# One fused attention and ELU kernel: four PSUM tiles for the first layer of batch 0, full-width stationary blocks, and issues in other slots

## The chip, the cores and the metric

The kernel runs on one core of a Trainium2 chip. Its time is device microseconds of one execution: 360.8 us is the median of three runs (360.18 to 362.03). Lower is better. The engines are PE (TensorE matmuls; PEld are its weight loads), DVE (VectorE), ACT (ScalarE), POOL (GpSimd) and SP (which here only issues DMAs).

## The reference: what is computed

```python
B, H, S, D = 8, 8, 576, 64                 # q, k, v
scores = q @ k.T / sqrt(D) - slope[h] * |i - j|     # slope[h] = 2 ** -(h + 1)
scores = where((i - j >= 0) & (i - j < 128), scores, -1e9)
attn = softmax(scores)                     # exp / sum
x = (attn @ v) as [B*S = 4608, H*D = 512]  # tokens x model
h = x @ w_in                               # [4608, 2048]
g = where(h > 0, h, exp(min(h, 0)) - 1)    # ELU
out = g @ w_out                            # [4608, 512], float32
```

Each query sees itself and the 127 keys before it, so attention is a band: 128 keys meet at most 256 queries.

## The kernel before

Everything runs on PE in float16 with float32 sums. The program is one long list of instructions in an order written out by hand; each engine takes its own instructions in that order and waits on semaphores for the others. The order comes from a loop over **slots** (L430): in slot s stand first what `before(s, ...)` has put there (exponentials on ACT), then `hidden(s)`, then `elu(s-1)`, then what `at(s, ...)` has put there (attention steps, loads, transposes), then `output` if the slot has one.

Attention of batch b (576 positions, 8 heads) is cut into key blocks u = 0 to 3 of 128 keys, of which the last also takes the 64 keys of block 4:

- `load_qk`, `load_v`, `load_wi`, `load_wo` issue DMAs on POOL's queue (they cast to float16); the first two load a batch, the others the weights.
- `turn_qk` transposes q and k on DVE (`QT`, `KT`). Batch 0 is done by `turn_first` instead: PE transposes into PSUM, copied out by DVE (k) and ACT (q).
- `scores(b, u)` multiplies key block u (stationary) with its 256 queries into `sp`, one PSUM tile of four banks, two heads a bank. For u = 3 it takes 192 queries for block 3 and then 64 for block 4, whose stationary block is 64 wide. In batch 0 the ALiBi bias is added by further matmuls (`SI`, `RB`); in the others the exponentials are multiplied by a table.
- `expo` takes exp from `sp` to `EX` on ACT; `weigh` multiplies `EX` with `TAB` on DVE (not in batch 0).
- `values(b, i, gp)` multiplies the weights of query block i (stationary, from `EX`) with `VP`, four heads at a time, into `av`; a column of ones in `VP` gives the denominator. DVE takes its reciprocal (L197) and multiplies (L198) into `xn`. Query block 4 has 64 queries, so there the stationary block is 64 wide, and one of its two parts has 64 rows.
- `turn` transposes `xn` into `xT`, by PE and DVE (batches 0 and 1 for the most part) or by a DMA of SP's queue.

The two layers take 512 tokens t at a time. `hidden(t, c0, w, f0, nf)` fills one PSUM bank `hp` with 512 columns of the first layer (16 matmuls with 128 tokens, 8 with 256), ACT takes exp into `e` (L230), POOL clips it (L231), and `elu` on DVE makes `g` from `e` and `hp` (L238), after which the bank is free. `hp` has two buffers, taken in turn by all of `hidden`. `output(t, ts, f0)` adds four matmuls of the second layer (128 tokens x 512) to a bank `op`; after the fourth such step ACT copies it to `ob` (three buffers) and SP stores it.

Slots 0 to 15 are `hidden` of t = 0 together with batch 0's attention, slots 16 and 17 the first 64 tokens of t = 1, slots 18 to 33 `output` of t = 0 with no `hidden` at all, slots 34 to 47 the rest of t = 1 with batch 1's attention; from there on each slot has a `hidden` and an `output`. Batch b from 2 on starts at slot `START[b]` (41, 57, 75, 93, 111, 129); its `values(b, 4, 0)` and `values(b, 4, 1)` stand 17 and 18 slots later, its `turn_qk` in the 8 slots before it starts.

PSUM's eight banks: four for `sp`, two for `hp`, one for `av` (also used as `output`'s ts = 1 in t = 0), one for `op` (also `xps`).

## Time and profile before

| | |
|---|---|
| median of three runs | 360.8 us (360.18 to 362.03) |
| the profiled execution | 360.57 us, of which the span on the page is 358.8 |
| PE busy | 332.8 us (93%), 3706 matmuls |
| DVE, ACT, POOL busy | 223.3 (62%), 175.4 (49%), 172.8 us (48%) |
| `hidden` on PE (L225) | 1600 matmuls |
| `output` on PE (L247) | 576 matmuls |
| `values` on PE (L189) | 576 matmuls, 128 of them with a 64-wide stationary block |
| `scores` on PE (L167, batches 1 to 7) | 560 matmuls, 112 of them with a 64-wide one |

How the rows are read. A row of a timeline is: start in us, busy us, engine, line, operation, out<-in, the stationary block (rows*columns), the shape, a count of equal instructions merged, and in brackets how long the engine had been idle before and what ended that. Matmuls are pipelined and the ends are modelled: eight matmuls merged can show 1.04 us and the next row start 0.87 us after this one, so a cost on PE is the distance between starts. A row of stretches gives busy time with the number of instructions for PE, PEld, DVE, ACT and POOL, then the clock granted to TensorE, the mean busy share of the DMA engines, and GB/s.

### The profile page before, as it was taken

What the parts mean: (1) busy time and instruction counts of PE and PEld (TensorE: products, weight loads), DVE (VectorE), ACT (ScalarE), POOL (GpSimd) and SP (SyncE); (2) the same over time, 40 slices, a digit from 0 to 9 for tenths busy, and PEclk for the clock granted to TensorE, in tenths of its full rate; (3) what the DMA queues carried; (4) which work ended last, traced back from release to release, by engine and by line L of the source; (5) the groups of instructions that cost most, each with busy time, mean ns of one, the idle gap of its engine ahead of it and who ended that gap; (6) DMA issues with size and microseconds to landing.
All of it is one profiled execution on the core that took longest, in us unless ns stands there. A gap on an engine that the chain in (4) does not pass through costs nothing.

```text
span 358.8 us, 8891 instructions
## 1 busy us (share of the span) xinstructions
PE 332.8 (93%) x3706; PEld 230.7 (64%) x3706; DVE 223.3 (62%) x443; ACT 175.4 (49%) x313; POOL 172.8 (48%) x261
## 2 busy tenths in 40 slices
PE   8898879856999999999999999999999999999994
PEld 8687664445676666766667666666677666666641
DVE  5445536479668866786669756786679566654320
ACT  1645344554455545554666255555556365533421
POOL 9336459254466536562666456562656133332320
PEclk9879999999999999999999999999999999999999
DMA  9998349995577838994899649991999311111011
GB/s 111 195 188 110 36 41 134 190 151 38 65 107 94 91 64 104 107 97 69 93 112 94 78 67 123 100 98 39 136 115 102 61 45 46 46 45 38 29 60 58
DMA packets 97320, 32.10 MB, mean 89 GB/s; under 512 B 87040, under 2 KB 92672, under 8 KB 97280
## 3 DMA queue, kind: packets, MB, share of 16 engines
q0 software_dynamic: 76480, 18.36, 60.2%
q1 hardware_dynamic: 20800, 13.18, 13.1%
q8 instruction: 29, 0.48, 0.5%
q14 instruction: 11, 0.09, 0.1%
HBM read 36.70 MB, written 9.44 MB: 129 GB/s over the span
## 4 chain that ended last, share of the span: by engine, by line
PE 68%; DVE 10%; ACT 8%; DMA 4%; issue 4%; POOL 4%; ACTq 0%; DVEq 0%; POOLq 0%
PE hp L225 26%; PE op L247 25%; PE av L189 9%; DVE g L238 5%; ACT EX L173 5%; PE sp L167 4%; POOL e L231 3%; ACT e L230 3%; DMA wo<-in_moe_w_out_dram 2%; DMA out_dram<-ob 2%; PE spare L257 2%; DVE EX L179 2%; DVE KT L127 1%; PE sp L148 1%; DVE QT L127 1%
## 5 line engine op out<-in xcount | busy, mean ns | idle before, releaser
L231 POOL TENSOR_SCALAR e<-e 128x512 f32<-128x512 f32 x144 | 93.5, 650 | 167.1 <-ACT e L230 166.3
L225 PE MATMUL hp<-xT,wi 128*128 128x256 f16 (+3 forms) x1600 | 151.0, 243 | 12.8 <-DVE g L238 9.4
L225 PEld LDWEIGHTS <-wi 128*128 128x128 f16 x1600 | 122.3, 98 | 52.4 <-issue 17.3
L247 PE MATMUL op<-wo,g 128*128 128x512 f16 x576 | 145.3, 379 | 2.6 <-ACT ob L251 1.4
L230 ACT ACTIVATE e<-hp 128x512 f32<-128x512 f32 x144 | 87.2, 605 | 115.0 <-PE hp L225 112.6
L238 DVE SCALAR_TENSOR_TENSOR g<-e,hp 128x512 f16<-128x512 f32 x144 | 96.9, 673 | 55.9 <-POOL e L231 54.4
L247 PEld LDWEIGHTS <-g 128*128 128x128 f16 x576 | 50.7, 97 | 48.2 <-issue 7.8
L173 ACT ACTIVATE EX<-sp 128x512 f16<-128x512 f32 (+1 forms) x121 | 69.8, 634 | 15.9 <-PE sp L167 10.1
L179 DVE TENSOR_TENSOR EX<-EX,TAB 128x1024 f16<-128x1024 f16 x56 | 39.1, 699 | 29.5 <-ACT EX L173 29.5
L189 PE MATMUL av<-VP,EX 128*128 128x65 f16 (+1 forms) x576 | 44.4, 200 | 2.5 <-ACT EX L173 1.3
L189 PEld LDWEIGHTS <-EX 128*128 128x128 f16 (+1 forms) x576 | 34.7, 100 | 12.6 <-issue 3.1
L251 ACT COPY ob<-op 128x512 f32<-128x512 f32 x36 | 21.1, 586 | 40.6 <-PE op L247 38.4
L198 DVE TENSOR_TENSOR xn<-av,rden 128x256 f16<-128x256 f32 (+1 forms) x80 | 33.8, 423 | 2.7
L93 POOL DMA_DIRECT2D VP<-in_v_dram x40 | 35.0, 879 | 0.7 <-issue 0.6
L197 DVE RECIPROCAL rden<-av 128x4 f32<-128x4 f32 (+1 forms) x80 | 14.1, 176 | 24.1 <-PE av L189 23.9
L127 DVE STREAM_TRANSPOSE KT<-st 128x576 f16<-128x576 f16 x28 | 22.5, 814 | 0.0
L127 DVE STREAM_TRANSPOSE QT<-st 128x576 f16<-128x576 f16 x28 | 22.3, 807 | 0.0
L167 PE MATMUL sp<-QT,KT 32*128 32x256 f16 (+2 forms) x560 | 18.3, 250 | 2.7 <-ACT EX L173 2.7
L87 POOL DMA_DIRECT2D st<-in_q_dram x28 | 19.1, 681 | 2.7 <-DMA wo<-in_moe_w_out_dram 2.1
L87 POOL DMA_DIRECT2D st<-in_k_dram x28 | 19.2, 689 | 0.7 <-DMA VP<-in_v_dram 0.6
L167 PEld LDWEIGHTS <-KT 32*128 32x128 f16 (+1 forms) x560 | 10.5, 95 | 5.9 <-issue 4.2
L257 PE MATMUL spare<-ident 128*128 128x128 f16 x90 | 6.6, 249 | 1.6 <-DVE ident L282 1.6
(33 smaller groups left out, 60.8 us busy)
## 6 DMA issues: line engine op xcount, KB each, us to landing
out_dram<-ob SPq DMA_DIRECT2D x36, 256.0 KB, 2.4
VP<-in_v_dram POOLq DMA_DIRECT2D x32, 128.0 KB, 4.0
st<-in_k_dram POOLq DMA_DIRECT2D x28, 144.0 KB, 3.6
st<-in_q_dram POOLq DMA_DIRECT2D x28, 144.0 KB, 3.5
wi<-in_moe_w_in_dram POOLq DMA_DIRECT2D x4, 512.0 KB, 11.1
wo<-in_moe_w_out_dram POOLq DMA_DIRECT2D x4, 512.0 KB, 6.1
VP<-in_v_dram POOLq DMA_DIRECT2D x8, 64.0 KB, 3.2
xT<-xn SPq DMA_TRANSPOSE x32, 3.4
```

The source lines that it names most:

```text
L87: nc.gpsimd.dma_start(st[b][32 * g:32 * g + 32, w, :, :, :, :].rearrange("p h n j d -> p (h n) (j d)"), (q, k)[w][b, 2 * g:2 * g + 2, :, : ...
L93: nc.gpsimd.dma_start(VP[b % 2][0:p, n, :, 0:D], v[b, :, 128 * n:128 * n + p, :].rearrange("h p d -> p h d"))
L127: V.transpose(o, st[b][:, w, h2, :, :, 32 * dh:32 * dh + 32])
L167: nc.tensor.matmul(sp[0:m, g, 256 * h2 + o:256 * h2 + o + n], kt[r, h2, dh, 128 * kb:128 * kb + m], qt[r, h2, dh, q0:q0 + n], start=dh == ...
L173: nc.scalar.activation(unit(b, u)[:, g0:g1, :, c0:c1], sp[:, g0:g1, :].rearrange("p g (h c) -> p g h c", h=2)[:, :, :, c0:c1], AF.Exp, sca ...
L179: V.tensor_tensor(out=e, in0=e, in1=TAB[:, int(u == 3), 2 * gp:2 * gp + 2, :, :], op=ALU.mult)
L189: nc.tensor.matmul(a[0:m, g, h2, :], e[0:kk, 2 * gp + g, h2, c:c + m], VP[b % 2][0:kk, n, 4 * gp + 2 * g + h2, 0:D + 1], start=j == 0, sto ...
L225: nc.tensor.matmul(p[:, l * w + u0:l * w + u1], w_in_sb[:, c, fc * 128:(fc + 1) * 128], xT[:, c, x0:x0 + u1 - u0], start=(c == 0), stop=(c ...
L230: nc.scalar.activation(e[:, 0:n], p[:, 0:n], AF.Exp)
L231: nc.gpsimd.tensor_scalar(out=e[:, 0:n], in0=e[:, 0:n], scalar1=1.0, scalar2=0.0, op0=ALU.min, op1=ALU.max)
L238: V.scalar_tensor_tensor(out=gs[t][:, f0:f0 + nf, c0:c0 + w], in0=sh(es.pop((t, c0, f0))), scalar=1.0, in1=sh(hps.pop((t, c0, f0))), op0=A ...
L247: nc.tensor.matmul(o, gs[t][:, fc, ts * 128:(ts + 1) * 128], w_out_sb[:, fc, :], start=(fc == 0), stop=(fc == NFC - 1))
```

## The change

It has four parts, all in the program's text below.

1. **PSUM.** `sp` becomes a two-bank tile `spa` and two one-bank tiles; `hp` becomes two named tiles. `hidden` is told its tile: in slots 0 to 3 `hp[0]` and `hp[1]` in turn, in slots 4 to 15 those two and `sp[2]`, `sp[3]`, four in turn, in slots 16 and 17 `sp[2]` and `sp[3]`. In slots 34 to 39 three in turn (`hp[0]`, `hp[1]` and the one of `op`), after that two as before. `e` has six buffers instead of three. Batch 1's PE transposes of `turn` use the bank of `av` instead of that of `op`.
2. **Batch 0's scores by four heads.** `first_scores(u, half, d)` does four heads into two banks, and `first_expo` takes their exponentials in pieces, one of 512 elements or two of 256, instead of one of 1024.
3. **Stationary blocks all 128 wide.** `KT` and `EX` are 64 columns longer and zeroed there, `VP`'s rows 64 to 127 of block 4 are zeroed, and `scores` and `values` always take 128 rows or columns. The rows that are not wanted are not read.
4. **Other slots.** The second part of `turn_first` (96 transposes) goes from the prologue into slot 0; block 1's scores are in front of slot 0's `hidden`; `load_wo(0)` and `load_wo(1)` follow the last `load_wi` in the prologue, `load_wo(2)` and `load_wo(3)` stand in slots 15 and 16, batch 1's loads a little earlier.

```diff
-    ps_h = ctx.enter_context(tc.tile_pool(name="ps_h", bufs=2, space=PSUM))
+    ps_h = ctx.enter_context(tc.tile_pool(name="ps_h", bufs=1, space=PSUM))
...
-    KT = [one([128, 2, 2, S], F16, f"KT{i}") for i in range(2)]
+    kt_ = [one([128, 4 * S + 64], F16, f"KT{i}") for i in range(2)]
+    KT = [t[:, 0:4 * S].rearrange("p (a b s) -> p a b s", a=2, b=2) for t in kt_]
-    EX = [one([128, 4, 2, 256], F16, f"EX{i}") for i in range(4)]
+    ex_ = [one([128, 2048 + 64], F16, f"EX{i}") for i in range(4)]
+    EX = [t[:, 0:2048].rearrange("p (g h c) -> p g h c", g=4, h=2) for t in ex_]
-    sp = ps_s.tile([128, 4, 512], F32, name="sp", tag="sp")
+    spa = ps_s.tile([128, 2, 512], F32, name="spa", tag="spa")
+    sp = [spa[:, 0, :], spa[:, 1, :]] + [ps_s.tile([128, 512], F32, name=f"sp{i}", tag=f"sp{i}") for i in (2, 3)]
+    hp = [ps_h.tile([128, 512], F32, name=f"hp{i}", tag=f"hp{i}") for i in range(2)]
...
+        def blocks(u):
+            return [(0, u, 128 * u, 256)] if u < 3 else [(0, 3, 384, 192), (192, 4, 512, 64)]
+        def first_scores(u, half, d):
+            heads = [(x, hh) for x in (2 * half, 2 * half + 1) for hh in range(2)]
+            for part, (o, kb, q0, n) in enumerate(blocks(u)):
+                for x, hh in heads:
+                    c = 256 * (x % 2) + o
+                    nc.tensor.matmul(sp[2 * d + hh][:, c:c + n], SI[:, 4 * hh + x, :], RB[:, 0:n],
+                                     start=part == x % 2 == 0, stop=False, skip_group_check=True)
+            for o, kb, q0, n in blocks(u):
+                for x, hh in heads:
+                    r, c = slice(64 * hh, 64 * hh + 64), 256 * (x % 2) + o
+                    k0 = x * S + 128 * kb
+                    nc.tensor.matmul(sp[2 * d + hh][:, c:c + n], kt_[0][r, k0:k0 + 128], Q0[r, x, q0:q0 + n],
+                                     start=False, stop=True, skip_group_check=True)
+        def first_expo(u, half, d, c0, c1):
+            if d == 0:
+                nc.scalar.activation(
+                    unit(0, u)[:, half::2, :, c0:c1],
+                    spa.rearrange("p g (h c) -> p g h c", h=2)[:, :, :, c0:c1], AF.Exp, scale=0.125)
+                return
+            for hh in range(2):
+                nc.scalar.activation(
+                    unit(0, u)[:, half + 2 * hh, :, c0:c1],
+                    sp[2 + hh].rearrange("p (h c) -> p h c", h=2)[:, :, c0:c1], AF.Exp, scale=0.125)
...
         def scores(b, u):
+                            k0 = (2 * h2 + dh) * S + 128 * kb
-                                sp[0:m, g, 256 * h2 + o:256 * h2 + o + n], kt[r, h2, dh, 128 * kb:128 * kb + m],
+                                sp[g][:, 256 * h2 + o:256 * h2 + o + n], kt_[b % 2][r, k0:k0 + 128],
         def values(b, i, part):
-                        nc.tensor.matmul(
-                            a[0:m, g, h2, :], e[0:kk, 2 * gp + g, h2, c:c + m],
-                            VP[b % 2][0:kk, n, 4 * gp + 2 * g + h2, 0:D + 1],
+                    for j, (u, c, n) in enumerate(parts):
+                        c += 512 * g + 256 * h2
+                        nc.tensor.matmul(a[:, x, h2, :], ex_[u][:, c:c + 128], VP[b % 2][:, n, 2 * g + h2, 0:D + 1],
...
-            e = es[t, c0, f0] = work.tile([128, 512], F32, name="e", tag="e")
+            e = es[t, c0, f0] = work.tile([128, 512], F32, name="e", tag="e", bufs=6)
...
+            V.memset(VP[i][64:128, 4, :, 0:D], 0.0)
+            V.memset(kt_[i][:, 4 * S:4 * S + 64], 0.0)
+        for e in ex_:
+            V.memset(e[:, 2048:2112], 0.0)
...
+        load_wo(0)
+        load_wo(1)
...
+        BUF = [hp[0], hp[1], sp[2], sp[3]]
+            HID[s] = [(0, 128 * sub, 128, 4 * f, 4, BUF[s % 2 if s < 4 else s % 4])]
+            HID[16 + f] = [(1, 0, 64, 8 * f, 8, BUF[2 + f])]
+            HID[s] = [(1, *step, (hp[0], hp[1], None)[(s - 34) % 3] if s < 40 else BUF[s % 2])]
+                HID[16 * t + 16 + j] = [(t, 256 * (j // 8), 256, 2 * (j % 8), 2, BUF[j % 2])]
...
+        at(0, turn_first, 1, 1, 0, hp[1])
+        at(0, values, 0, 1, 0)
+        at(0, turn_first, 0, 1, 0, None)
...
-        at(0, load_wo, 0)
-        at(2, load_wo, 1)
-        at(17, load_wo, 2)
-        at(18, load_v, 1, 0)
-        at(19, load_v, 1, 1)
-        at(20, load_wo, 3)
-        for n in range(3):
-            at(21 + n, load_v, 1, 2 + n)
+        at(15, load_wo, 2)
+        at(16, load_wo, 3)
+        for n in range(5):
+            at(17 + n, load_v, 1, n)
```

Three places in the built order. First PE at the end of `values(2, 4, 0)` and the `output` behind it, as at every batch's query block 4 (`EX_92` is key block 3's weights, `VP_87` the even batches' values); of the eight pairs the last three stand here. Before:

```order
L189 LDWEIGHTS EX_92
L189 MATMUL av<-VP_87,EX_92 64x65
L189 LDWEIGHTS EX_92
L189 MATMUL av<-VP_87,EX_92 64x65
L247 LDWEIGHTS g
L247 MATMUL op<-wo,g 128x512
```

After:

```order
L206 LDWEIGHTS EX_92
L206 MATMUL av<-VP_87,EX_92 128x65
L206 LDWEIGHTS EX_92
L206 MATMUL av<-VP_87,EX_92 128x65
L267 LDWEIGHTS g
L267 MATMUL op<-wo,g 128x512
```

Nothing moved here; the outputs have 128 rows instead of 64, the same eight matmuls stand in the same place.

Second DVE from slot 9 to slot 18, where `elu` frees the tiles of `hidden` (`hp_99` and `hp_100` are the two of `hp`, `sp_97` and `sp_98` the two taken from the scores). Before:

```order
L238 SCALAR_TENSOR_TENSOR g<-e,hp 128x4x128
L197 RECIPROCAL rden<-av 64x4
L198 TENSOR_TENSOR xn<-av,rden 64x256
L238 SCALAR_TENSOR_TENSOR g<-e,hp 128x4x128
L211 COPY xT<-xps 128x4x64
L238 SCALAR_TENSOR_TENSOR g<-e,hp 128x4x128 x7
L238 SCALAR_TENSOR_TENSOR g<-e,hp 128x8x64 x2
```

After:

```order
L227 COPY xT<-xps 128x4x64
L257 SCALAR_TENSOR_TENSOR g<-e,sp_98 128x4x128
L257 SCALAR_TENSOR_TENSOR g<-e,hp_99 128x4x128
L257 SCALAR_TENSOR_TENSOR g<-e,hp_100 128x4x128
L257 SCALAR_TENSOR_TENSOR g<-e,sp_97 128x4x128
L257 SCALAR_TENSOR_TENSOR g<-e,sp_98 128x4x128
L257 SCALAR_TENSOR_TENSOR g<-e,sp_97 128x8x64
L257 SCALAR_TENSOR_TENSOR g<-e,sp_98 128x8x64
```

The last copy of batch 0's `turn` has gone from before seven to before five steps of t = 0, these steps take four tiles in turn, and the two of 64 tokens take the same two tiles as the two steps ahead of them.

Third ACT at the start, from the copies of q to the first exponentials of `hidden` (`EX_89` to `EX_91` are key blocks 0 to 2). Before:

```order
L123 COPY QT_83<-tp 128x2x384 x2
L173 ACTIVATE EX_89<-sp 128x4x128 x2
L173 ACTIVATE EX_89<-sp 128x8x128
L123 COPY QT_83<-tp 128x4x192
L173 ACTIVATE EX_90<-sp 128x8x128 x2
L230 ACTIVATE e<-hp 128x512
L173 ACTIVATE EX_91<-sp 128x8x128
```

After:

```order
L130 COPY QT_83<-sp_98 128x2x384
L167 ACTIVATE EX_89<-spa 128x2x2x128
L172 ACTIVATE EX_89<-sp_97 128x2x128
L172 ACTIVATE EX_89<-sp_98 128x2x128
L167 ACTIVATE EX_89<-spa 128x2x2x128
L172 ACTIVATE EX_89<-sp_97 128x2x128
L172 ACTIVATE EX_89<-sp_98 128x2x128
L167 ACTIVATE EX_90<-spa 128x2x2x128
L172 ACTIVATE EX_90<-sp_97 128x2x128
L172 ACTIVATE EX_90<-sp_98 128x2x128
L249 ACTIVATE e<-hp_99 128x512
L130 COPY QT_83<-tp 128x4x192
```

The third copy of q has gone from between blocks 0 and 1 to behind the first exponential of `hidden`, and each half of a block is three instructions instead of one or two.

More of the change, by code (lines that the diff above doesn't have):

```diff
@@ L163, in scores @@
+        def scores(b, u):
+            for o, kb, q0, n in blocks(u):
                 for h2 in range(2):
@@ new lines, in values @@
+            if part == 0:
+                xnt[b, i] = work.tile([128, 4, 2, D], F16, name="xn", tag="xn", bufs=6)
+            o = xnt[b, i][0:m, part::2, :, :] if b == 0 else xnt[b, i][0:m, 2 * part:2 * part + 2, :, :]
+            r = work.tile([128, 2, 2], F32, name="rden", tag="rden", bufs=2)
+            V.reciprocal(out=r[0:m], in_=a[0:m, :, :, D])
+            V.tensor_tensor(out=o, in0=a[0:m, :, :, 0:D], in1=r[0:m].unsqueeze(3).broadcast_to([m, 2, 2, D]),
+                            op=ALU.mult)
@@ L348 @@
                 OUT[16 * t + 26 + j] = (t, j // 4, 4 * (j % 4))
+        at(0, turn_first, 1, 1, 0, hp[1])
+        at(0, values, 0, 1, 0)
+        at(0, turn_first, 0, 1, 0, None)
         at(0, values, 0, 1, 1)
-        at(0, scores, 0, 2)
-        before(1, expo, 0, 2, 0, 4, 0, 128)
+        for half in range(2):
+            before(1, first_expo, 1, half, half, 128, 256)
         at(1, turn, 0, 1, False)
-        before(2, expo, 0, 2, 0, 4, 128, 256)
-        at(2, values, 0, 2, 0)
-        at(3, values, 0, 2, 1)
@@ L358 @@
[L358 to L367 removed]
+        at(1, first_scores, 2, 0, 0)
+        at(1, first_scores, 2, 1, 1)
+        before(2, first_expo, 2, 0, 0, 0, 128)
+        before(2, first_expo, 2, 1, 1, 0, 128)
@@ L432 @@
                 f(*a)
-            if s in HID:
-                hidden(*HID[s])
-            if s - 1 in HID:
-                elu(*HID[s - 1])
+            for step in HID.get(s, []):
+                hidden(*step)
+            for step in HID.get(s - 1, []):
+                elu(*step)
             for f, a in tasks.get(s, []):
```

165 lines of the change are left out of this document (70 added, 95 removed).

## The prediction

> **What bounds the kernel now.** I read the table by slices first, then stretches of 5 and 50 us, then the timelines of TensorE and of whoever it waited for, stretch by stretch. A slot below is one turn of the slot loop; slot s begins with `hidden(s)`, and its start is read from the first matmul of `hidden` on PE.
>
> ```profile
> PE   8898879856999999999999999999999999999994
> 15.00:20.00 5.00, 4.42 (x43) 3.22 (x42) 1.14 (x4) 1.97 (x3) 0.00 (x0) 0.50 1.79 184
> 40.00:45.00 5.00, 3.20 (x49) 2.84 (x49) 2.30 (x4) 2.12 (x4) 2.53 (x5) 1.00 0.31 30
> 80.00:85.00 5.00, 3.80 (x116) 3.09 (x113) 4.93 (x11) 2.85 (x6) 3.22 (x5) 1.00 0.90 60
> 150.00:200.00 50.00, 49.67 (x525) 34.04 (x523) 38.22 (x76) 27.85 (x50) 28.23 (x43) 1.00 0.97 95
> ```
>
> Columns of the last four: stretch, its length, busy PE, weight load, DVE, ACT, POOL, the granted clock, DMA share, GB/s. Two regimes. From about 92 us to 330 us PE is busy 49.67 of 50 us, so a microsecond taken off PE there comes off the end, as long as nobody else is as full; DVE has 38.22. Before 92 us PE has holes: at 40 to 45 us it is busy 3.20 of 5 with every other engine under 2.6, a chain of latencies; at 80 to 85 us DVE is full (4.93). At 15 to 20 us the clock was at half.
>
> **The narrow stationary blocks.** `values(b, 4, ·)` has 64 queries and so a stationary block 64 wide. One such boundary in the PE timeline, and `scores(b, 3)` beside `scores(b, 0)`:
>
> ```profile
> 160.07 1.04 PE L225 MATMUL hp<-xT,wi 128*128 128x256 f16 x8
> 160.94 0.41 PE L189 MATMUL av<-VP,EX 128*128 128x65 f16 x8
> 161.19 1.02 PE L247 MATMUL op<-wo,g 128*128 128x512 f16 x4
> 162.05 1.04 PE L225 MATMUL hp<-xT,wi 128*128 128x256 f16 x8
> 163.01 1.24 PE L189 MATMUL av<-VP,EX 128*64 128x65 f16 x8
> 164.18 1.04 PE L247 MATMUL op<-wo,g 128*128 128x512 f16 x4
> 167.19 0.61 PE L167 MATMUL sp<-QT,KT 32*128 32x256 f16 x16
> 167.74 1.04 PE L247 MATMUL op<-wo,g 128*128 128x512 f16 x4
> 152.36 0.76 PE L167 MATMUL sp<-QT,KT 32*128 32x192 f16 x32
> 153.05 1.04 PE L247 MATMUL op<-wo,g 128*128 128x512 f16 x4
> ```
>
> Starts count, since busy times overlap. Eight matmuls with 128-wide blocks hold PE from 160.94 to 161.19, 0.25 us; the same eight of `values(b, 4, ·)` (half of them 64 wide on 128 rows, half on 64) from 163.01 to 164.18, 1.17 us: 31 against 146 ns each, though both stream 65 columns. Going in costs too: `hidden` to `values` takes 0.96 us there and 0.87 at 160.07. After the change all eight have exactly the form of 160.94 (128 rows, 128 columns, 65 streamed), so the price is measured, not guessed: 1.17 − 0.25 + 0.09 = 1.01 us each. There are two a batch; those of batches 1 to 7 lie in the PE-bound regime: 14 × 1.01 = **14.1 us** (term A). Batch 0's two lie in the next part.
>
> Is DVE ready for it? Behind the boundary it waits for these very matmuls:
>
> ```profile
> 164.29 0.17 DVE L197 RECIPROCAL rden<-av 64x4 f32<-64x4 f32 x1 [0.70 <-PE av L189]
> 165.55 0.64 DVE L238 SCALAR_TENSOR_TENSOR g<-e,hp 128x512 f16<-128x512 f32 x1
> 167.30 0.17 DVE L197 RECIPROCAL rden<-av 64x4 f32<-64x4 f32 x1 [1.11 <-PE av L189]
> 168.62 1.04 PE L225 MATMUL hp<-xT,wi 128*128 128x256 f16 x8
> ```
>
> The `hidden` at 168.62 would come two microseconds earlier, at 166.6, and needs the `hp` that DVE frees with the step at 165.55, which ends at 166.2 and itself starts 0.7 us sooner once the idle 0.70 closes. It fits, so I count A in full.
>
> The Trainium skill (TensorE: Matmul & The Clock Gate, "Weight-path perf modes") says a fast weight load is used when a block has 128 columns and is not FP32, so the 64-wide ones would not get it; the trace agrees on which are slow. Its formula of columns ÷ 1.2 ns, with 32 cycles for the fast load, would estimate 53 against 27 ns, hence 14 × 8 × 26 ns = 2.9 us for A; the rows say 146 against 31, and the rows decide.
>
> `scores(b, 3)`: 0.69 us against 0.55. Its 32 matmuls stream the same columns in total as those 16, and four stand side by side in both. With one width, 0.14 is the least that I expect and I take 0.2, six times (batches 2 to 7): **1.2 us** (B; ends 0 and 1.8).
>
> **Batch 0's first layer, slots 10 to 17.** With two `hp` buffers, slot s waits until DVE has emptied slot s−2:
>
> ```profile
> 40.01 1.05 PE L225 MATMUL hp<-xT,wi 128*128 128x128 f16 x16
> 41.80 1.05 PE L225 MATMUL hp<-xT,wi 128*128 128x128 f16 x16 [0.74 <-DVE g L238]
> 42.89 0.60 ACT L230 ACTIVATE e<-hp 128x512 f32<-128x512 f32 x1 [1.20 <-PE hp L225]
> 43.57 0.61 POOL L231 TENSOR_SCALAR e<-e 128x512 f32<-128x512 f32 x1 [1.19 <-ACT e L230]
> 44.22 0.69 DVE L238 SCALAR_TENSOR_TENSOR g<-e,hp 128x512 f16<-128x512 f32 x1 [1.11 <-POOL e L231]
> 51.27 1.09 PE L225 MATMUL hp<-xT,wi 128*128 128x64 f16 x32 [0.70 <-DVE g L238]
> 52.20 2.97 PE L247 MATMUL op<-wo,g 128*128 128x512 f16 x13
> 29.50 1.96 PE L225 MATMUL hp<-xT,wi 128*128 128x128 f16 x32 [0.52 <-DVE xT L211]
> ```
>
> The chain PE, ACT, POOL, DVE takes 3.16 us from 41.80, so 1.58 a slot; slots 10 to 17 take 52.20 − 40.01 = 12.2. Four tiles give 0.79 a slot, and PE's own 0.9 (two slots back to back took 1.96 at 29.50; 0.93 from 51.27 to 52.20) is then the longer. Slots 10 to 15: 6 × 0.9 plus 0.45 for a `values` and a `turn` that move in = 5.9. But slots 16 and 17 write the tiles of 14 and 15 again, so slot 16 starts 3.16 after slot 14, not 1.8: 1.35 more. Sum 5.9 + 1.8 + 1.35 = 9.1 us, and **3.0 us** gained (C).
>
> **The head, slots 0 to 9**, 18.12 to 40.01 before:
>
> ```profile
> 12.32 1.88 PE L115 MATMUL tp<-ident,s 32*64 32x32 f16 x96
> 14.24 0.80 ACT L123 COPY QT<-tp 128x768 f16<-128x768 f16 x1 [0.80 <-PE tp L115]
> 18.12 1.90 PE L225 MATMUL hp<-xT,wi 128*128 128x128 f16 x16
> 26.78 1.19 PE L148 MATMUL sp<-RB,SI 128*128 128x192 f16 x16
> 27.91 0.74 PE L157 MATMUL sp<-QT,KT 64*128 64x192 f16 x16
> L173 ACT ACTIVATE EX<-sp 128x512 f16<-128x512 f32 x114 | 62.9, 610 | 11.0 <-PE sp L167 10.1 <-PE sp L157 0.7
> L173 ACT ACTIVATE EX<-sp 128x1024 f16<-128x1024 f32 x7 | 7.1, 1022 | 4.9 <-PE sp L157 4.9
> ```
>
> The 96 transposes at 12.32 and the ACT copy behind them move from in front of the scores of block 1 to behind `hidden(0)`, so slot 0 can begin about 2.3 us earlier, near 15.8; the same work then stands between slots 0 and 1, as do now the scores of blocks 2 and 3. From 1022 and 610 ns a 256-element exponential is about 0.4, so a half unit (610 + 2 × 400) costs ACT 0.4 us more than the one of 1022; that is done six times, in blocks 0 to 2. PE's own work in slots 0 to 9: ten times 0.9 (as in C), transposes 1.9, the scores of block 3 another 1.9 (26.78 and 27.91) and of block 2, half as many matmuls, 1.3, seven `values` at 0.25, turns 0.8, 16.7 in all; I add 2.5 for the half clock (half of the five microseconds that it shows) and 2 for waits on ACT (its six times 0.4 over): 21.2, to 37.0, 3.0 earlier than 40.01. Half a microsecond kept back for the landing of the first weights, I take **2.5 us** (D; ends: a loss of 1, if a full 3.4 us more runs at half clock and ACT is late, and a gain of 6 by PE's work alone). The eight memsets more on DVE lie beside the 90 warm-up matmuls and cost nothing; were they late, they would hold up the first scores and D with them.
>
> The skill (same page, "PE-mode transpose") says transposes do not count as PE-busy for the clock. The half clock at 15 to 20 us follows the 96 transposes, which agrees; by that rule the low clock may move to 18 to 25 us, worth the loss end of D.
>
> **Slots 18 to 33 and the loads.**
>
> ```profile
> 59.68 1.89 PE L247 MATMUL op<-wo,g 128*128 128x512 f16 x8 [0.41 <-DMA wo<-in_moe_w_out_dram]
> 64.61 1.02 PE L247 MATMUL op<-wo,g 128*128 128x512 f16 x4 [0.67 <-DMA wo<-in_moe_w_out_dram]
> 66.28 7.83 SPq L252 DMA_DIRECT2D out_dram<-ob  x4
> 73.17 0.58 ACT L251 COPY ob<-op 128x512 f32<-128x512 f32 x1 [2.18 <-DMA out_dram<-ob]
> 74.31 0.62 PE L167 MATMUL sp<-QT,KT 32*128 32x256 f16 x16 [2.47 <-ACT EX L173]
> 90.58 1.05 PE L225 MATMUL hp<-xT,wi 128*128 128x128 f16 x16 [0.26 <-DVE g L238]
> ```
>
> `load_wo(2)` and `load_wo(3)` stand two and four slots earlier on POOL's queue, ahead of all five `load_v`: the waits of 0.41 and 0.67 go. The fourth `ob` copy waits 2.18 us for the first store, which shares the DMA engines with batch 2's loads; that backlog starts about 3 us earlier against slot 18, so about half of the wait goes. 1.1 + 1.2 = **2.3 us** (E; ends 0 and 4). Slots 34 to 41, 74.31 to 90.58, are DVE's stretch with the same DVE steps in the same order: the third tile there buys **0**, and the 16.3 us stay (ends ±1).
>
> **Sum.** 14.1 + 1.2 + 3.0 + 2.5 + 2.3 = 23.1 us off. The profiled execution took 360.57 us with a span of 358.8 (1.8 outside it), 0.2 under the median of 360.8: 360.57 − 23.1 = **337.5 us**.
>
> **Rivals.** *The loads eat the head.* The same bytes must land before slot 33 in fewer microseconds; the store of 7.83 us shows how full the engines are there. Against it: at 40 to 45 us the DMA share is only 0.31. If C, D and E all vanish, 15.3 stay: 345.3. *DVE becomes the bound at the boundaries*: its work per batch is unchanged and nearly fills the stretch before 163 us, so half of A could be lost: 344.5. Against it: the 0.70 and 1.11 us of waiting on PE. *Width is not what is slow*: were it something the change leaves as it is, only loads differ; then A is near 0 and the time 351. Against it: 160.94 has every property that the new blocks get. *Slower than before*: the half clock of 15 to 20 us stays through batch 0, since the transposes and small scores are spread through it. Half clock costs at most 0.5 us per microsecond; it decides only after 46 us more of it, so from 20 to beyond 66 us, giving some 361 to 363. Against it: the clock was back at 1.00 by 40 us though PE was busy only 64%.
>
> **How the numbers follow.** Forecast 0.70, with a range of its own of 332 to 342 (D and E at their ends, half of a microsecond on C); loads 0.12; DVE 0.12; width 0.02; clock 0.02; the rest 0.02 between these. The range 331.5 to 345 leaves out the last ones and part of the first rival. About 0.5%, 1.8 us, is what a measurement here can tell from no change; only the clock rival gets there: faster 0.96, same 0.02, slower 0.02.
>
> **What would show it.** Right: eight `av` matmuls of 128 columns in about 0.25 us at every batch boundary, slot starts near 0.9 us apart in slots 8 to 15 with one wait of over a microsecond at slot 16, no PE wait on `wo`, and slots 34 to 41 still 16 us with DVE full. Wrong: new PE waits on DVE at each boundary, a granted clock of 0.50 beyond 25 us, or the stretch up to slot 42 ending later than 84 us.

## The result and the profile after

The changed kernel takes **339.6 us** (median of 4 runs, 339.08 to 340.11), the kernel before in the same session 360.51: a ratio of 0.9412, with a 95% interval of 0.9379 to 0.9445. The forecast was 337.5, range 331.5 to 345. The profiled execution took 339.08 us with a span of 337.3. Profiled once more later (run e9, 340.38 us median of 6, ratio 0.9398, 0.9362 to 0.9435) the same kernel showed a span of 339.5. Starts of slots, read from the first matmul of `hidden` (slot 18: of `output`), in us:

| | slot 0 | 10 | 18 | 34 | 42 | end |
|---|---|---|---|---|---|---|
| before | 18.12 | 40.01 | 52.20 | 70.54 | 90.58 | 358.8 |
| changed | 16.14 | 36.96 | 46.59 | 63.51 | 83.50 | 337.3 |
| changed, second trace (e9) | 16.25 | 39.14 | 48.78 | 65.70 | 85.84 | 339.5 |

So of 21.5 us in the spans 7.1 are won before slot 42 and 14.4 behind it. The table by slices and four stretches of the changed kernel:

```profile
PE   8887989786999999999999999999999999999994
PEclk9999999989999999999999999999999999999999
```

```profile
15.00:20.00 5.00, 4.28 (x133) 3.34 (x132) 1.52 (x4) 2.53 (x5) 1.35 (x2) 1.00 1.49 195
40.00:45.00 5.00, 3.79 (x79) 3.67 (x77) 3.09 (x7) 2.39 (x4) 4.31 (x8) 1.00 0.31 30
75.00:80.00 5.00, 2.89 (x71) 2.48 (x68) 4.93 (x12) 2.55 (x5) 1.97 (x4) 1.00 0.92 57
150.00:200.00 50.00, 49.85 (x509) 34.17 (x506) 37.84 (x76) 28.43 (x52) 26.89 (x42) 1.00 0.81 92
```

The regime behind 92 us is unchanged (PE 49.85 of 50, DVE 37.84): fewer microseconds of PE are wanted there, and they came off the end. The stretch at 40 to 45 us now has POOL at 4.31 of 5 where nobody was over 3.20, and DVE still fills 75 to 80 us (4.93). A batch boundary, and DVE behind it:

```profile
150.00 1.03 PE L267 MATMUL op<-wo,g 128*128 128x512 f16 x4
150.86 1.04 PE L244 MATMUL hp<-xT,wi 128*128 128x256 f16 x8
151.74 0.41 PE L206 MATMUL av<-VP,EX 128*128 128x65 f16 x8
151.98 1.02 PE L267 MATMUL op<-wo,g 128*128 128x512 f16 x4
152.84 1.04 PE L244 MATMUL hp<-xT,wi 128*128 128x256 f16 x8
153.72 0.41 PE L206 MATMUL av<-VP,EX 128*128 128x65 f16 x8
154.05 0.28 PE L183 MATMUL spa<-QT,KT 32*128 32x256 f16 x2
```

```profile
152.24 0.16 DVE L212 RECIPROCAL rden<-av 64x4 f32<-64x4 f32 x1
154.16 0.17 DVE L212 RECIPROCAL rden<-av 64x4 f32<-64x4 f32 x1
```

The two steps of `values(b, 4)`, at 151.74 and 153.72, hold PE for 0.24 us before the `output` that follows and for 0.33 before the `scores` that follows; the forecast read 0.25 off a step with `output` behind it. No row carries a wait on DVE, and the reciprocals of 64 queries no longer wait 0.70 and 1.11 us for `av`. Batch 0's slots 10 to 18:

```profile
36.96 1.06 PE L244 MATMUL sp<-xT,wi 128*128 128x128 f16 x16
38.10 1.05 PE L244 MATMUL sp<-xT,wi 128*128 128x128 f16 x16
39.43 1.96 PE L244 MATMUL hp<-xT,wi 128*128 128x128 f16 x32
41.23 1.95 PE L244 MATMUL sp<-xT,wi 128*128 128x128 f16 x32
44.39 1.09 PE L244 MATMUL sp<-xT,wi 128*128 128x64 f16 x32 [1.21 <-DVE g L257]
45.67 1.09 PE L244 MATMUL sp<-xT,wi 128*128 128x64 f16 x32 [0.19 <-DVE g L257]
46.59 1.03 PE L267 MATMUL op<-wo,g 128*128 128x512 f16 x4
```

Up to slot 15 the slots stand 0.9 to 1.3 us apart, and the one long wait is at slot 16, 1.21 us for the tile of slot 14. No row of PE between slots 18 and 42 carries a wait on `wo`. Two more rows, ACT's and PE's, from between slots 34 and 35:

```profile
65.87 0.58 ACT L271 COPY ob<-hp 128x512 f32<-128x512 f32 x1 [1.91 <-DMA out_dram<-ob]
67.00 0.26 PE L183 MATMUL sp<-QT,KT 32*128 32x256 f16 x1 [1.98 <-ACT EX L189]
```

The wait on the first store is nearly all there (2.18 before), and PE's wait behind it too.

### The profile page after: what moved, and what is told of

The parts are those of the page before. It is cut to its first block, busy times and chain, and to the rows that moved or that the text cites. A ratio compares the mean times of both kernels' runs of the same rounds, so it can differ in the third digit from the quotient of the medians.

```text
span 337.3 us, 8925 instructions
## 1 busy us (share of the span) xinstructions
PE 314.4 (93%) x3706; PEld 221.5 (66%) x3706; DVE 223.1 (66%) x451; ACT 176.4 (52%) x326; POOL 174.8 (52%) x261
## 3 DMA queue, kind: packets, MB, share of 16 engines
q1 hardware_dynamic: 20800, 13.18, 13.6%
## 4 chain that ended last, share of the span: by engine, by line
PE 69%; DVE 10%; ACT 8%; DMA 4%; issue 4%; POOL 3%; ACTq 0%; DVEq 0%; POOLq 0%
PE op L267 26%; PE hp L244 26%; PE av L206 5%; DVE g L257 4%; ACT EX L189 4%; PE spa L183 4%; POOL e L250 3%; DMA xT<-xn 3%; ACT e L249 2%; PE spare L277 2%; DMA out_dram<-ob 2%; DVE EX L194 2%; PE hp L267 2%; DVE KT L134 2%; PE sp L244 1%
## 5 line engine op out<-in xcount | busy, mean ns | idle before, releaser
L250 POOL TENSOR_SCALAR e<-e 128x512 f32<-128x512 f32 x144 | 95.5, 663 | 140.6 <-ACT e L249 139.6
L244 PE MATMUL hp<-xT,wi 128*128 128x256 f16 (+3 forms) x1392 | 140.2, 249 | 4.3 <-DVE g L257 1.6
L267 PE MATMUL op<-wo,g 128*128 128x512 f16 x528 | 134.3, 379 | 1.4 <-ACT ob L271 1.4
L249 ACT ACTIVATE e<-hp 128x512 f32<-128x512 f32 x134 | 81.3, 606 | 93.0 <-PE hp L244 90.2
L257 DVE SCALAR_TENSOR_TENSOR g<-e,hp 128x512 f16<-128x512 f32 x134 | 90.4, 675 | 51.7 <-POOL e L250 50.7
L206 PE MATMUL av<-VP,EX 128*128 128x65 f16 x576 | 30.9, 194 | 6.8 <-DVE xn L213 4.1
L189 ACT ACTIVATE EX<-spa 128x512 f16<-128x512 f32 x56 | 30.5, 600 | 8.6 <-PE sp L183 4.5
L206 PEld LDWEIGHTS <-EX 128*128 128x128 f16 x576 | 26.9, 98 | 9.7 <-ACT e L249 2.8
L189 ACT ACTIVATE EX<-sp 128x512 f16<-128x512 f32 x56 | 31.4, 620 | 0.0
L212 DVE RECIPROCAL rden<-av 128x4 f32<-128x4 f32 (+1 forms) x80 | 14.1, 176 | 8.1 <-PE av L206 7.8
L183 PE MATMUL spa<-QT,KT 32*128 32x256 f16 (+2 forms) x280 | 17.6, 250 | 0.0
## 6 DMA issues: line engine op xcount, KB each, us to landing
wi<-in_moe_w_in_dram POOLq DMA_DIRECT2D x4, 512.0 KB, 11.2
wo<-in_moe_w_out_dram POOLq DMA_DIRECT2D x4, 512.0 KB, 11.2
```

The lines of the kernel that those rows point to most:

```text
L183: nc.tensor.matmul(sp[g][:, 256 * h2 + o:256 * h2 + o + n], kt_[b % 2][r, k0:k0 + 128], QT[b % 2][r, h2, dh, q0:q0 + n], start=dh == 0, st ...
L189: nc.scalar.activation(unit(b, u)[:, g, :, :], sp[g].rearrange("p (h c) -> p h c", h=2), AF.Exp, scale=0.125)
L206: nc.tensor.matmul(a[:, x, h2, :], ex_[u][:, c:c + 128], VP[b % 2][:, n, 2 * g + h2, 0:D + 1], start=j == 0, stop=j == len(parts) - 1)
L244: nc.tensor.matmul(p[:, l * w + u0:l * w + u1], w_in_sb[:, c, fc * 128:(fc + 1) * 128], xT[:, c, x0:x0 + u1 - u0], start=(c == 0), stop=(c ...
L249: nc.scalar.activation(e[:, 0:n], p[:, 0:n], AF.Exp)
L250: nc.gpsimd.tensor_scalar(out=e[:, 0:n], in0=e[:, 0:n], scalar1=1.0, scalar2=0.0, op0=ALU.min, op1=ALU.max)
```

## The experiments

The code cuts are shortened. Ratios are against the kernel before, run beside each. Four sessions gave 360.5 to 361.8 us for it, so times of different sessions are compared by ratio. Where a trace decides, the reference for slots 10 to 42 is 45.66 to 45.81 us: e3, e4 and e8 have the changed kernel's tiles, order and loads and differ in `values(b, 4)` alone (slots 10 to 18 take 9.62 to 9.74 us in them, 9.63 in the changed kernel). The changed kernel's own traces take 46.54 and 46.70 there, with a half clock near 70 us that those three have not.

**What is slow about `values(b, 4)`: e1 to e4, and e8.** All are the changed kernel with the eight matmuls of that step altered (L206); `m` is 64 there. The two properties that the change altered together are taken apart.

```diff
 e1: both back
+ kk = 64 if n == 4 else 128
- matmul(a[:, x, h2, :], ex_[u][:, c:c + 128], VP[b % 2][:, n, ...])
+ matmul(a[0:m, x, h2, :], ex_[u][0:kk, c:c + m], VP[b % 2][0:kk, n, ...])
 e2: rows alone back
+ matmul(a[:, x, h2, :], ex_[u][0:kk, c:c + 128], VP[b % 2][0:kk, n, ...])
 e3: columns alone back
+ matmul(a[0:m, x, h2, :], ex_[u][:, c:c + m], VP[b % 2][:, n, ...])
 e4: 96 columns, all rows
+ matmul(a[0:96, x, h2, :], ex_[u][:, c:c + 96], VP[b % 2][:, n, ...])
```

e1: 

> The changed kernel with values(b, 4) narrow again as before: 64 stationary columns, and 64 rows for key block 4; scores stay wide. Width theory (a stationary block of fewer than 128 columns is what is slow): the eight av matmuls of a narrow step take 1.17 us instead of 0.25, 14 steps in the PE-bound stretch at about 1.0 each give 13.7, batch 0's two half a microsecond each at most: 339.6 + 13.7 to 14.7 = 353.3 to 354.3 us. Rival (most of the gain after slot 42 came from somewhere else, such as the six buffers of e): under 346 us.

e2: 

> The changed kernel with 128 stationary columns everywhere, but key block 4 multiplied with its 64 rows only, so that 128-row and 64-row blocks alternate as before. Width theory: as fast as the changed kernel, 339.6 +- 0.7 us, eight matmuls in 0.25 us. Rows theory (the alternation of 128 and 64 rows was what made each block wait): 1.17 us for the eight and 353 us. Both: in between.

e3: 

> The changed kernel with all 128 rows but 64 stationary columns in values(b, 4). Width theory: 1.17 us for the eight av matmuls and 353 to 354 us. Rows theory: 0.25 us and 339.6. By the load's length alone (half the columns to load) it would be no slower than the changed kernel.

e4: 

> As with 64 stationary columns, but 96 of them. If exactly 128 columns get the quick load, 96 is as slow as 64 or slower by the 32 more columns: 1.17 to 1.4 us for the eight and 353 to 357 us. If the cost falls as the block comes nearer to full width: halfway, about 0.7 us and 346 us.

Measured: e1 354.59 us (ratio 0.982, 0.977 to 0.9871), e2 351.35 (0.9721, 0.9639 to 0.9804), e3 342.92 (0.9502, 0.9454 to 0.955), e4 340.49 (0.9429, 0.9365 to 0.9493). Against the changed kernel's 0.9412 and 360.5 us that is 14.7, 11.1, 3.2 and 0.6 us more, each with an interval of 2 to 3 us to either side. The traces say it more closely: from the matmul ahead of the eight to the one that follows them, summed over the fourteen steps of batches 1 to 7, the four kernels take 13.9, 11.2, 2.7 and 1.4 us more than the changed kernel. The width is the small part; the rows are the large one. So e1 came out near what the width theory had for it, and e2 in between, near the rows theory. e3 and e4 met none of what was expected of them: e3 is faster than the width theory and slower than the rows theory, and e4 is faster than both of its guesses. One step in e2 and one in e3, with the row that follows:

```profile
159.79 1.14 PE L207 MATMUL av<-VP,EX 128*128 128x65 f16 x8
160.85 0.28 PE L183 MATMUL spa<-QT,KT 32*128 32x256 f16 x2
```

```profile
153.36 1.04 PE L244 MATMUL hp<-xT,wi 128*128 128x256 f16 x8
154.33 0.44 PE L206 MATMUL av<-VP,EX 128*64 128x65 f16 x8
154.70 1.04 PE L267 MATMUL op<-wo,g 128*128 128x512 f16 x4
```

With 128 columns throughout and rows of 128 and 64 in turn (the row shows the shape of the first), the eight of e2 take 1.06 us; e3's, 64 columns wide with all rows, take 0.37. Taken from the starts of single matmuls, this is the time in ns from each of the eight to the next one (the last figure to the step that follows, ahead of them the last `hidden` matmul to the first of the eight). It is one step of each; the medians of the twelve steps of batches 2 to 7 (for the last figure, of the eight that `output` follows) agree within 2 ns:

```
              in   1   2   3   4   5   6   7   8->next
changed      109  29  35  29  29  29  30  34   29   (output)
e1 both      202 148 144 147 145 147 144 148  146   (output)
e2 rows      109 126 134 137 133 137 133 137  133   (output)
e3 columns   203  52  36  29  30  36  29  34  126   (output)
e4 96 cols   109  29  44  45  45  45  45  45   45   (output)
e8 grouped   109  29  35  32 126  39  36  33  122   (output)
```

A matmul does not take the 146 ns for being narrow or short. Every change of the block's shape class from one matmul to the next costs some 0.1 us: in e3 there are two, on entering (203 instead of 109) and on leaving (126 instead of 29), with 29 to 52 between them; in e2 there are eight, one behind each matmul. The Trainium skill has the rule on a page that the forecast did not use, TensorEngine Tiling (Array Packing), "Key Properties": a change of tiling mode, as between 128 and 64 rows, drains TensorE. The changes between its modes of 128 and 64 rows, and of 128 and 64 columns, are the ones that the table shows as slow, and 96 columns, which fit no smaller mode, show none; the page gives no figure, the gaps about 0.1 us. The page does not say that a plain matmul with a short or narrow block runs in such a mode, and no trace shows what TensorE does in the 0.1 us, so that the two are the same thing is inferred from the pattern. That it is the change and not the short block itself needed one more run, e8: the matmuls of e2 in another order, the four of 128 rows first (the flag `start` moves with them, to the very first of the eight).

```diff
+ for j, (u, c, n) in enumerate(parts):      # block 3, then block 4
+     for x, g in enumerate(banks):
+         for h2 in range(2):
+             matmul(a[:, x, h2, :], ex_[u][0:kk, ...], VP[b % 2][0:kk, n, ...],
+                    start=j == x == h2 == 0, stop=j == 1)
```

> The changed kernel with 64 rows in key block 4 of values(b, 4) again (128 columns, as the earlier run that took 351.35 us), but the eight matmuls of one step in another order: first the four of 128 rows, then the four of 64 rows, so one change of rows in the step and one on leaving it, not seven. If the change of rows from one matmul to the next is what is slow (about 0.1 us each), the eight take 0.35 to 0.5 us instead of 1.07, and the time is 342 to 344 us. Rival, each 64-row block is slow by itself (its load, its empty half): the eight still take about 1.07 us and the time is 351 us. A third: only the 64-row half is slow, at about 0.13 us each, 0.65 us for the eight: 345 to 346.

Measured: 341.41 us, ratio 0.945 (0.9424 to 0.9477), nearly 10 us less than e2 with the same matmuls in another order, and a little under the 342 that was expected. The eight take 0.45 us, with two slow gaps (126 and 122 ns), and the 64-row blocks follow each other in 33 to 39 ns. The first theory stands, and both rivals fall. Nearly all that the rows cost was to be had by the order alone, without making a block taller.

**The widths alone: e5**, the kernel before with 128 columns in every block of `scores` and `values`, 128 rows in those of `values`, the longer and zeroed buffers that this takes, and nothing else of the change.

```diff
- m = 128 if kb < 4 else 64
+ m = 128
- e[0:kk, 2 * gp + g, h2, c:c + m], VP[b % 2][0:kk, n, ...]
+ ex_[u][:, c:c + 128], VP[b % 2][:, n, ...]
```

> The kernel before with the widths alone changed: every stationary block of scores and values 128 columns and 128 rows. Tiles, order of slots, exponentials and loads as before. If terms A and B of the sum stand by themselves (measured between the two traces: fourteen steps of about 0.98 us and six of 0.13, 14.5 us in all), about 346 us (345 to 347), with slot 42 starting near 90 us as before and the boundaries about 2 us shorter each. Rival, the widths pay only together with the new slots (DVE or a tile then holds PE up at the boundaries): 349 or more, with a PE wait on DVE of over 0.5 us behind each values(b, 4).

Measured: 348.1 us, ratio 0.9615 (0.9589 to 0.9641), 13.9 us off, with an interval of 13.0 to 14.9. In its trace slot 42 starts at 92.32 (a half clock from 75.7 to 79.1 us lies ahead of it), and from there to the end of the span (346.8) it is 254.5 us: 268.2 before, 253.8 in the changed kernel. So terms A and B need no other part of the change. As it stands 348.1 lies between the two expectations; its ratio on the 360.5 us of the first session gives 346.6, inside the first, and no PE wait on DVE over 0.5 us stands behind a `values(b, 4)`, which the rival wanted.

**Four tiles or two: e6, e7.** e6 puts all of batch 0's first layer on `hp0` and `hp1`; e7 only slots 16 and 17.

```diff
 e6
- HID[s] = [(0, 128 * sub, 128, 4 * f, 4, BUF[s % 2 if s < 4 else s % 4])]
+ HID[s] = [(0, 128 * sub, 128, 4 * f, 4, BUF[s % 2])]
 e6 and e7
- HID[16 + f] = [(1, 0, 64, 8 * f, 8, BUF[2 + f])]
+ HID[16 + f] = [(1, 0, 64, 8 * f, 8, BUF[f])]
```

e6: 

> The changed kernel, with all of batch 0's first layer (and slots 16 and 17) on hp0 and hp1 in turn, so two tiles. Theory (term C: the chain PE, ACT, POOL, DVE of 3.16 us over two tiles gives 1.58 a slot): slots 10 to 17 take about 12 us instead of 9.63, slot 18 starts 2 to 3 us later (48.6 to 49.6), and the end moves by the same, 341.6 to 342.6. Rival, what follows swallows it (loads and the store of the output then have had time to land, and the 1.9 us wait on that store goes): slot 42 within 0.7 us of 83.5 and the end within 0.7 us of 339.6.

e7: 

> The changed kernel, with slots 16 and 17 in hp0 and hp1 (last used by slots 12 and 13) instead of the tiles of slots 14 and 15. Theory (the 1.21 us wait at slot 16 is that reuse, and everything to slot 18 is one chain): the wait goes, slot 18 starts about 1.2 us earlier (45.4), and 0.5 to 1.2 us come off the end (338.4 to 339.1). Rival, the backlog of transfers sets what comes next: the wait on the first output store grows by what was won, slot 42 stays at 83.5 within 0.3 us and the end at 339.6.

In e6 PE waits for DVE again, at six of the slots 10 to 17; three of them:

```profile
46.24 1.05 PE L244 MATMUL hp<-xT,wi 128*128 128x128 f16 x16 [0.33 <-DVE g L257]
48.01 1.05 PE L244 MATMUL hp<-xT,wi 128*128 128x128 f16 x16 [0.72 <-DVE g L257]
49.40 1.09 PE L244 MATMUL hp<-xT,wi 128*128 128x64 f16 x32 [0.33 <-DVE g L257]
```

46.24 to 49.40 is 3.16 us for two slots, the chain of the forecast to the hundredth. Slots 10 to 18 take 12.18 us (39.92 to 52.10) against 9.63, so 2.55 more. Its fourth copy waits only 0.82 us for the store where the references wait 1.9 to 2.0, and slots 10 to 42 take 47.03 us, 1.3 more than the references: half of the loss is swallowed by that wait. The time, 342.41 us, ratio 0.9461 (0.9427 to 0.9495), is by the ratios some 1.8 us over the changed kernel, with intervals that just overlap. The theory has the place and the size, the rival half of what follows.

e7: 339.23 us, ratio 0.9367 (0.9339 to 0.9394), some 1.6 less than the changed kernel by ratios, with overlapping intervals again. In the trace slots 10 to 18 take 7.93 us instead of 9.63 (1.7 won, 1.21 and 0.19 of it the waits), but slots 18 to 34 take 17.89 instead of 16.92, since the outputs `op` of the third and fourth row block use `hp0` and `hp1` next, which slots 16 and 17 have only just filled. Slots 10 to 42 come to 44.00, 1.7 under the references, with a shorter wait on the store. The new waits on DVE:

```profile
49.16 1.02 PE L267 MATMUL hp<-wo,g 128*128 128x512 f16 x4 [0.29 <-DVE g L257]
50.55 1.02 PE L267 MATMUL hp<-wo,g 128*128 128x512 f16 x4 [0.36 <-DVE g L257]
```

The time, 339.23 us, lies between the two expectations and decides for neither. One reason stands behind slot 42, where this trace takes 255.23 us to the end and the changed kernel 253.77. PE waits there for the DMA transposes of `turn` (`xT`), 2.00 us in all against 0.63; the longest:

```profile
213.02 1.03 PE L244 MATMUL hp<-xT,wi 128*128 128x256 f16 x8 [1.01 <-DMA xT<-xn]
```

The kernel before has no such wait. Of the traces with wide blocks e12 has none either, and it has the same tiles as e7, so the tiles are not the reason; which execution gets how much of it, no run here explains.

**Loads and the store: e9 to e12**, beside each other. e9 is the changed kernel itself; e10 has the loads back in their slots; e11 has one `ob` buffer more; e12 is e7 and e11 together.

```diff
 e10
- at(15, load_wo, 2); at(16, load_wo, 3); at(17 + n, load_v, 1, n) for n in 0..4
+ at(17, load_wo, 2); at(18, load_v, 1, 0); at(19, load_v, 1, 1)
+ at(20, load_wo, 3); at(21 + n, load_v, 1, 2 + n) for n in 0..2
 e11, e12
- ob = work.tile([128, DO], F32, name="ob", tag="ob")
+ ob = work.tile([128, DO], F32, name="ob", tag="ob", bufs=4)
```

e9: 

> The changed kernel once more, unaltered, beside the next three. In its first trace the half clock stood at 67 to 71 us; in every other kernel with the same head it stood once for 3.4 us between 20 and 25 us. If that place is the usual one, slot 10 starts near 39.0 us instead of 36.96 (half of the 3.4 us and a later start of 0.8), slot 42 near 84 us, and the time is 340 to 341.5 us. Rival, the head runs at full clock as in the first trace: slot 10 at 37.0 and 339 to 340 us.

e10: 

> The changed kernel with load_wo(2), load_wo(3) and the load_v of batch 1 in their slots of before (17, 20; 18, 19, 21 to 23). Theory (term E's first part, 1.1 us): PE waits on wo come back, 0.4 to 1.6 us each, and the end is 0.5 to 1.7 us later than the changed kernel's. Rival, the loads' place doesn't matter since the wait on the store of output follows anyway: the end within 0.4 us of the changed kernel's.

e11: 

> The changed kernel with four buffers for ob instead of three, so that the fourth copy of output tile 0 needs no store to have landed. Theory (term E's second part: the copy, and scores(1, 2) behind it, wait 1.9 us on that store and nothing else is due): ACT's wait on out_dram goes, PE's wait of 1.98 us at scores(1, 2) falls under 0.5, and the end is 1 to 1.9 us earlier. Rival, DVE is the bound right behind it (4.9 of 5 us from 70 us on), so that what is won is waited for on DVE: the end within 0.4 us of the changed kernel's.

e12: 

> Both together: slots 16 and 17 in hp0 and hp1, and four ob buffers. If each stall is a link of one chain up to slot 42, the gains add: 1.4 to 1.8 for the slots and 1 to 1.9 for the buffer, so 2.4 to 3.5 us less than the changed kernel. Rival, one wins what the other would have (the shorter first layer already shortened the wait on the store to 0.97 us, so only that is left for the fourth buffer): 1.5 to 2.4 us less. If DVE's stretch swallows it: under 1 us.

e9, 340.38 us: its head is slower by 2.2 us at slot 10 with the same instructions in the same order, and its clock column says why:

```profile
15.00:20.00 5.00, 5.00 (x126) 3.84 (x126) 0.90 (x2) 1.70 (x4) 1.36 (x2) 0.70 1.48 195
20.00:25.00 5.00, 4.15 (x52) 3.11 (x47) 2.77 (x8) 2.52 (x6) 0.61 (x1) 0.66 1.51 198
70.00:75.00 5.00, 4.67 (x65) 4.27 (x60) 4.13 (x10) 3.53 (x7) 3.37 (x6) 0.74 0.47 49
```

The half clock stands twice in the head and once around 70 us; in the first trace it stands only at the last of these places. The first expectation has the place in the head (slot 10 at 39.14, for 39.0) and the time (340 to 341.5); slot 42 it has 1.8 us too early (85.84, for 84), as it reckoned with one stretch and three came. The head at full clock, which the rival expected, is what the first trace and e11 show and this one does not.

e10, 340.3 us, ratio 0.9414 (0.937 to 0.9458): not told apart from e9, which by the times is what the rival expected. Its trace has the wait on `wo` back, and slots 18 to 34 take 18.64 us instead of 16.92:

```profile
61.42 1.02 PE L267 MATMUL oa<-wo,g 128*128 128x512 f16 x4 [1.28 <-DMA wo<-in_moe_w_out_dram]
70.07 0.26 PE L183 MATMUL sp<-QT,KT 32*128 32x256 f16 x1 [1.24 <-ACT EX L189]
```

The second row is where half of it is returned: the wait behind the store falls from 2.07 in e9 to 1.24. Slots 10 to 42 take 46.55 us, 0.8 over the references. That is in favour of the theory at its lower end, and too little for the times to show; the argument rests on the one trace.

e11, **336.38 us**, ratio 0.9303 (0.9275 to 0.9331), 4.0 us under e9 and clear of its interval; the fastest median here. The fourth copy no longer waits, and `scores(1, 2)` runs through. Its copies on ACT:

```profile
62.64 0.60 ACT L271 COPY ob<-hp 128x512 f32<-128x512 f32 x1
63.59 0.63 ACT L271 COPY ob<-hp 128x512 f32<-128x512 f32 x1
```

Slots 10 to 42 take 43.82 us, 1.9 under the references, which is the wait itself: DVE had not been the bound just behind it (2.48 of 5 us at 65 to 70 in the changed kernel), and the theory stands at its upper end. The 4.0 us of the times are more than was expected (1 to 1.9), and the rest is half clock for the most part. The traces of e9 and e11 differ by 2.4 us at slot 10 and by 1.0 in the stretch of 70 us, both where e9 has half clock and e11 has none. And over the six executions the granted clock is 0.9888 in the mean for e9 and 0.9953 for e11 (0.9942 for e10, 0.9937 for e12). That difference is 4.4 us at half clock out of some 338, which at 1.3 to 1.6 us lost for each 3.4 (below) is an estimated 1.7 to 2.1 us. Whether a buffer has anything to do with how often the clock halves, no run here shows; until one does, 1.9 us is what the buffer has been shown to give. By the same working e10 had 3.7 us less at half clock than e9, worth an estimated 1.5 us, and that may be what hides its loss.

e12, 337.22 us, ratio 0.9316 (0.9279 to 0.9353): not told apart from e11 by the times. Slots 10 to 42 take 42.82 us, 2.9 under the references, where the two alone had 1.7 and 1.9: that is inside what was expected if the gains add (2.4 to 3.5), though 0.7 us overlap. Its head has the half clock that e11's has not (slot 10 at 38.80 against 36.73), which hides it in the time.

## Why the prediction was right, and where not

**A (14.1 forecast, B 1.2).** Together they gave 14.4 behind slot 42 in the changed kernel and 13.7 in e5, against 15.3. The price of a step was read rightly, since both forms stood in the rows of before: in the changed kernel it is 0.24 + 0.11 on entering. From the matmul ahead of the eight to the one that follows them, the fourteen steps take 19.10 us before and 5.21 after, so A is 13.9; four of the steps win less, since `scores` follows them and its blocks of 32 rows cost a change in both kernels. B was sized at 0.2 a time and measured 0.13 (`scores(b, 3)` takes 0.56 instead of 0.69), 0.8 in all. Of these 14.7 some does not reach the end, and one reason is a wait of PE on the DMA transposes of `turn`, of which the trace of before has none. It is 0.63 us in the changed kernel's first trace, and 0.97 in e5, all in one place:

```profile
221.57 1.03 PE L227 MATMUL hp<-xT,wi 128*128 128x256 f16 x8 [0.97 <-DMA xT<-xn]
```

But the reason given, that narrow columns make a block slow, fell. The step of the forecast that failed is the sentence that read the 64 columns as the difference between 31 and 146 ns: the same eight matmuls differed in their rows too, and the forecast even says so, half on 128 rows and half on 64, without asking which of the two counts. By e2 and e3 the rows in turn are 11.1 us of it and the columns 3.2 (11.2 and 2.7 by the starts). So A came out right although its cause was wrong: the change swapped the whole slow form for the whole fast one, and for that sum the cause does not matter. The forecast's citation of the Trainium skill fell with it: the trace was said to agree with "Weight-path perf modes" (TensorE: Matmul & The Clock Gate) on which blocks are slow, but e2's blocks of 128 columns are slow all the same, while e3's of 64 run at 29 to 52 ns once inside the step. The estimate of 2.9 us from that page's figures happens to be near e3's 3.2, but the table of gaps puts that on entering and leaving, not on each load. The rival "width is not what is slow" had the right doubt and the wrong consequence, because the change removed the other property as well.

**C (3.0).** 9.63 us against 9.1, so 2.56. The wait at slot 16 was forecast at 1.35 and is 1.21; without it slots 10 to 15 take 6.2 us, where 5.9 were forecast with the `values` and the `turn` between them, and slots 16 and 17 take 2.2, for 1.8. e6 confirms the mechanism and its size of 2.55, and shows that half of it is taken back by the wait on the store before slot 42; the forecast had taken slot 18's gain for the end's.

**D (2.5).** 3.05 in the first trace, 0.87 in the second. Forecast was 21.2 us for slots 0 to 9 with 2.5 of half clock and 2 of waits; the first trace has 20.82 with no half clock and waits that add up to more than 3, of which these are the largest two:

```profile
20.43 0.41 PE L206 MATMUL av<-VP,EX 128*128 128x65 f16 x8 [1.15 <-ACT QT L130]
27.34 0.40 PE L206 MATMUL av<-VP,EX 128*128 128x65 f16 x8 [1.61 <-DVE xn L213]
```

So the sum came out near by two errors that cancel in that trace, which is luck; in the second the half clock is there and the gain is smaller. The 2.5 also came from too short a stretch: the five microseconds that the row of 15 to 20 us shows are part of 6.8 us in the trace of before, from 14.9 to 21.7, of which 3.2 lie ahead of slot 0. Slot 0 was forecast at 15.8 and starts at 16.14. The Trainium skill's rule on transposes and the clock was given as a reason for half clock at 18 to 25 us. Of twelve traces with the new head ten have a stretch that begins between 19.7 and 21.5 us, behind the transposes that stand between slots 0 and 1, and two have none there. In e5, whose transposes stand in the prologue as before (13.6 to 15.6 us), it begins at 21.1, more than five microseconds behind them. No run here varied the transposes alone, so the cause stays open.

**E (2.3) and slots 34 to 41 (0).** Slots 18 to 33 and the wait behind them gave 1.7, slots 34 to 41 took 0.2 more. Half of the wait on the store was to go; 0.3 of 2.18 went. And the part on `wo`, counted at 1.1, is worth 0.8 by e10's trace: what the earlier loads win, the wait on the store takes back in half. The term was mis-sized because it added two waits of which one stands behind the other: part of what the first gives up, the second takes. e11 shows the larger lever, a fourth `ob` copy that needs no store to have landed.

**Rivals.** DVE did not become the bound at the boundaries (no PE wait there). The loads did not eat the head: PE's waits in slots 0 to 9 are on ACT and DVE, none on a load. The 7.83 us that the forecast read as one store are four, issued at 66.28, 69.05, 70.52 and 73.78 and merged in one row, so that row says nothing of how full the engines were. The half clock did not last: never more than 6.8 us at a time.

**The signs of being wrong.** Two of those that the forecast named came up all the same. The granted clock was 0.50 beyond 25 us, at 67 to 71 us in the first trace and 69 to 73 in the second, and in the second slot 42 starts at 85.84, later than 84. The rival behind the first sign needed 46 us more of half clock and got 3.4 at that place; the forecast had no term for a half clock that comes and goes between executions.

**Sum.** 23.1 forecast; 21.5 between the first traces, 20.9 between the medians. The 1.6 missing from the former are A and B (0.9), E (0.8) and C (0.4), less what D gave over (0.5). Three smaller sums of the forecast are off and changed nothing: without A the time is 351.6, not 351; half of the wait of 2.18 is 1.1, not 1.2; and D and E at their ends with half a microsecond on C reach 343.8, not 342.

## What to carry to other kernels

Count the changes of a stationary block's shape class along PE's order, not the blocks: each between 128 and 64 rows or columns cost about 0.1 us here, so group matmuls of one shape or pad all to one. When two forms are compared for a price, write down every property in which they differ before naming the cause; the price holds if the change swaps one whole form for the other, and the cause does not. Time won ahead of a wait on a transfer can be taken back by that wait (half of it in e6 and e10), so remove the last wait of such a row first. When single microseconds are at stake, compare the granted clock of the executions too, and not only their times.

## What the runs showed of the hardware

A change between 128 and 64 rows, or 128 and 64 columns, from one matmul to the next costs 0.09 to 0.11 us; blocks of 96 columns cost 45 ns each instead of 30, with no such step. Going from `values` into `scores`, whose blocks have 32 rows, costs the same in both kernels (123 to 127 ns from the last `values` matmul to the first of `scores`, and 147 behind the four steps of the kernel before that have alternating rows; 29 where `output` follows a wide step), and the change left that in place.

The half clock comes in stretches of 3.4 us, or two end to end, in every trace before 92 us, but not at the same place in two executions of one kernel (15 to 18, 21 to 25 and 69 to 73 us in e9, 67 to 71 in the first trace). In the head one stretch costs 1.3 to 1.6 us from slot 1 to slot 4 (7.76 us in the first trace and 7.77 in e11 without one, 9.04 in e6 to 9.31 in e9 with one). The Trainium skill (TensorE: Matmul & The Clock Gate, "What's actually happening") says that a free-running window of 3.4 us sets the clock; the length and the varying place agree. It names a whole idle window as what lowers it, and here the clock fell with no wait of PE over 2.5 us ahead of it: PE was busy for 1.4 of the 3.4 us before the fall near 70 us, in both traces of the changed kernel.
